# Low bits of float64 weights converted on ScalarE, and a planner that costs instructions by their spacing: attention, feed-forward block and gated block on one Trainium2 core

## The chip, the cores and the metric

The kernel runs on one core of a Trainium2 chip. The metric is the device time of one execution in microseconds (us). The times come from three runs; the profile comes from one more execution.

## What is computed

Three blocks follow one another on a batch of 4 sequences of 448 tokens, with 768 features (12 heads of 64). The weights and inputs of the second and third block are float64 in part.

```python
# attention, per head
scores = cap * np.tanh(scale * np.matmul(q, k.transpose(0, 1, 3, 2)) / cap)
attn = np.exp(scores - np.max(scores, axis=-1, keepdims=True))
attn = attn / (np.sum(attn, axis=-1, keepdims=True) + 1e-09)
x = np.matmul(attn, v)                            # then heads side by side
# feed-forward block
xn = (x - mu) / np.sqrt(var + 1e-06) * g_ln
x = x + np.maximum(xn @ w_ch1, 0.0) @ w_ch2       # 768 -> 3072 -> 768
# gated block
h = np.maximum(x @ w_in, 0.0)                     # 768 -> 1024
u, v = (h[..., :d_ff // 2], h[..., d_ff // 2:])
v_s = np.einsum('ts,bsd->btd', w_spatial, (v - mu) / np.sqrt(var + 1e-06)) + b_spatial[None, :, None]
out = (u * v_s) @ w_out
```

Weights reach the chip as pairs of 32-bit words, a low one and a high one, of a float64 number. The kernel makes a float32 of each pair by itself. Products are made of float32 split into two parts (a rounded one and the rest), with three matmuls for one product.

## The kernel before

The work on the four sequences is done in two passes of two sequences. In time order: attention of sequences 0 and 1 (some 0 to 115 us); the first feed-forward matmul of these two, with the attention of sequences 2 and 3 in between and the conversion of `w1` and `w2` (to about 350 us); the second feed-forward matmul, `y_seven`, which works with seven products in place of eight (to about 500 us); the gated block (to about 625 us); and the same two blocks for sequences 2 and 3, with weights that the first pass has converted and kept in memory (to the end).

No queue is written out by hand. `Recorder` notes every operation with an engine, a cost and a latency, in a program order; `Program.edges` finds what depends on what; `Program.order` gives each operation a due time, counted back from the TensorE work that needs it; `Program.plan` simulates the five queues (TensorE, VectorE, ScalarE, GpSimd, and SyncE, which issues all DMAs) with these costs and takes, for a free engine, the ready operation that is due first and has its buffers. The order in which the simulation takes the operations is the order in which they are emitted, so a change of any cost reorders every queue. An operation noted under `either()` has a second engine. The second engine takes it (`k` is above 0 in `pick`) only if its cost there is no greater than the wait that the simulation sees at the first engine, plus a bias: `BIAS` = 0.1 us, and -0.8 where the second engine is VectorE.

The cost in `Recorder.__getattr__` is a fixed part plus columns by a rate: for ScalarE 0.16 us (0.13 from PSUM) and 1200 columns per us, for VectorE 0.14 us and 960 (1920 for copies and `tensor_scalar` outside PSUM); the latency of both is 0, and `DELAY` = 0.13 us is added to every hand-over.

The conversion stands in `value`. A raw tile holds `n` pairs; `hi` and `lo` are its odd and even words, read with a stride of 8 bytes. ScalarE makes a rebased float of the high word (`Prelu` with a negative slope that keeps the sign), VectorE shifts this left by three bits (tile `t` seen as integers, `ti`), and VectorE ors in the three highest bits of the low word. Four early tiles of `w1` are given a `home` and go another way, with the sign put in by a third VectorE step. The float32 tile is then stored for the second pass, and `weight` or `y_seven` split it into two parts. In the trace the raw tiles are `w` (`w6`, `w4` in the code) and `w6m`, the converted ones `wr`, `wc` and `wcm`, and the split ones `wh`, `whm` and the like; `wr` is 768 columns wide, `wc` 512, `wcm` either. `hs` and `rs` are an activation and its split. Every operation is recorded by one line, L533, so rows are told apart by tiles.

Of the kernel before, what the change touches and what calls it, by code (L numbers as in the profile page):

```python
# [10 lines left out]
F32 = mybir.dt.float32  # L11
F32R = mybir.dt.float32r
I32 = mybir.dt.int32
ACTF = mybir.ActivationFunctionType
ALU = mybir.AluOpType

# [31 lines left out]
BIAS = 0.1  # L48
# [8 lines left out]


REBASE = 2.0 ** -112

EARLY = 4


class View:
# [17 lines left out]
    def __getattr__(self, name):  # L82
        return getattr(self.at, name)
# [127 lines left out]
class Program:  # L211
# [137 lines left out]
    def plan(self, due):  # L349

        n = len(self.ops)
# [12 lines left out]
        out = []  # L364
# [8 lines left out]
        def room(i):  # L373
            need = {}
            for b in bufs[i]:
                if b.tile is None:
                    need.setdefault(b.pool, set()).add(b)
            key = [(p, p.changes) for p in need]
            if blocked.get(i) == key:
                return False  # L380
            if all(p.fits(new) for p, new in need.items()):
                return True
            blocked[i] = key
            return False

        def reach():
            return max(spent + AHEAD, relief)

        def pick(e):


            q = ready[e]
            skipped = []
            found = None
            while q and found is None:
                d, i, k = heapq.heappop(q)
                if taken[i]:
                    continue
                if d > reach():
                    skipped.append((d, i, k))  # L400
                    break
                if k:
                    alt = self.ops[i][0]
                    home = alt[0][0]
                    wait = max(0.0, free[home] - now) if busy[home] else 0.0
                    for d2, i2, k2 in ready[home]:
                        if not taken[i2] and (d2, i2) <= (d, i) and not k2:
                            wait += self.ops[i2][0][0][1]
                    if alt[k][1] > wait + (BIAS if e != 'V' else -0.8):
                        skipped.append((d, i, k))  # L410
                        continue
                if not room(i):
                    skipped.append((d, i, k))
                    continue
                found = i, k
            for x in skipped:
                heapq.heappush(q, x)
            return found
# [5 lines left out]
        while True:  # L424
            for e in ready:
# [5 lines left out]
                i, k = found  # L431
# [6 lines left out]
                cost, latency = self.ops[i][0][k][1:3]  # L438
# [3 lines left out]
                if e == "D":  # L442
                    moved = max(moved, now + 1.1) + latency
                    latency = moved + 0.77 - now - cost
# [49 lines left out]
class Recorder:  # L494
# [3 lines left out]
    def __getattr__(self, method):  # L498
        fn = getattr(self.engine, method)

        def put(a):
            return a.place() if isinstance(a, View) else a

        def record(*args, **kw):
            out = kw["out"] if "out" in kw else args[0]
            ins = [a for a in list(args) + list(kw.values()) if hasattr(a, "tensor") and a is not out]
            n = out.free_size()
            latency = 0.0
            psum_in = any(a.space == bass.MemoryType.PSUM for a in ins)
            if self.name == "PE":  # L510
                cost = (n / 2400 + 0.0133) * kw["rhs"].ap[0][1] / 128
                if kw["rhs"].dtype == F32:

                    part = kw["rhs"].ap[0][1] * kw["out"].ap[0][1] / 128 ** 2
                    cost = (4 * n / 2400 + 0.004) * part + (0.004 if part < 1 else 0.0)
            elif self.name == "D":
                cost, latency = 0.5, 4 * out.size() / 360e3
            elif self.name == "A":
                cost = (0.13 if psum_in else 0.16) + n / 1200
                cost += 0.094 if hasattr(kw.get("scale"), "tensor") else 0.0  # L520
            elif self.name == "P":
                cost = 1.0 if "pow" in repr(args) + repr(kw) else 0.45 + n / 500
            elif method == "reciprocal":
                cost = 0.15 + n / 160
            elif method in ("tensor_copy", "tensor_scalar") and not psum_in:
                cost = 0.14 + n / 1920
            else:
                cost = 0.14 + n / 960
            if self.name == "V":
                cost += 0.06 * sum(hasattr(kw.get(k), "tensor") for k in ("scalar", "scalar1", "scalar2"))  # L530

            def call():
                fn(*(put(a) for a in args), **{k: put(a) for k, a in kw.items()})  # L533

            self.program.add(self.name, cost, latency, call, [out], ins)

        return record
# [3 lines left out]
def attn_ffn_gmlp_kernel(  # L541
# [17 lines left out]
    V, A, P, T, SP = (prog.engines[n] for n in ("V", "A", "P", "PE", "D"))  # L559
# [19 lines left out]
    def slots(name, n, shape, dt, pool=const):  # L579
# [7 lines left out]

    shapes = {"rb": ([128, 2, DH], F32R), "w6": ([128, DM, 2], I32), "es": ([128, 2, S], F32),
              "qk": ([128, 2 * S], F32), "vt": ([128, 512], F32), "acc": ([128, S], F32),
              "r": ([128, 2, S], F32R), "wr": ([128, DM + 24], F32), "wh": ([128, 2, DM], F32R),  # L590
              "wa": ([128, 2, HK], F32R), "wq": ([128, DM], F32), "pad": ([128, 24], F32), "gap": ([128, 48], F32), "w4": ([128, DH, 2], I32)}
    protos = {n: dram.tile(s, dt, name=f"proto_{n}") for n, (s, dt) in shapes.items()}
# [60 lines left out]
    def cp(o, a, engines=None):  # L653

        with prog.either():
            for e in engines or (V, A):
                if e is A:
                    A.activation(out=o, in_=a, func=ACTF.Copy)
                else:
# [24 lines left out]
    def ahead(kind, j):  # L684

        with prog.early():
            value(kind, j, pool=raw6[1])

    def value(kind, j, home=None, pool=wr):

        n = width[kind]
        if kind == "ws":
            t = hs.get()
            SP.dma_start(out=t, in_=source[kind][j])
        elif (kind, j) in kept:
            t = pool.get()[:, 0:n]
            SP.dma_start(out=t, in_=kept[kind, j])
        else:
            raw = raw6[0 if n > DH else 2].get()[:, 0:n]
            SP.dma_start(out=raw.rearrange("p n t -> p (n t)"), in_=source[kind][j].bitcast(I32))  # L700
            t = pool.get()[:, 0:n]
            ti = t.bitcast(I32)
            hi, lo = raw[:, :, 1], raw[:, :, 0]
            if home is None:
                A.activation(out=t, in_=hi.bitcast(F32), func=ACTF.Prelu, scale=REBASE, alpha=-(2.0 ** 32))
            else:
                with prog.either():
                    for e in (V, A):
                        if e is A:
                            A.activation(out=t, in_=hi.bitcast(F32), func=ACTF.Copy, scale=REBASE)  # L710
                        else:
                            V.tensor_scalar(out=t, in0=hi.bitcast(F32), scalar1=REBASE, scalar2=None, op0=ALU.mult)
            V.tensor_scalar(out=ti, in0=ti, scalar1=3, scalar2=None, op0=ALU.logical_shift_left)
            if home is not None:
                V.scalar_tensor_tensor(out=ti, in0=hi, scalar=-(1 << 31), in1=ti, op0=ALU.bitwise_and,
                                       op1=ALU.bitwise_or)
            V.scalar_tensor_tensor(out=ti, in0=lo, scalar=29, in1=ti, op0=ALU.logical_shift_right,
                                   op1=ALU.bitwise_or)
            if kind == "w2":
                if j % KD == 0:  # L720
                    kept2.append(dram.tile([128, KD, n], F32, name=f"kept_{kind}_{j}"))
                d = kept2[j // KD][:, j % KD]
            else:
                d = dram.tile([128, n], F32, name=f"kept_{kind}_{j}")
            kept[kind, j] = d
            SP.dma_start(out=d, in_=t)
        return t
# [59 lines left out]
    def expo(sc, e):  # L787
        A.activation(out=e, in_=sc, func=ACTF.Tanh, scale=qsc)
        A.activation(out=e, in_=e, func=ACTF.Exp, scale=capt)
        return e  # L790
# [17 lines left out]
    def split_s(i, t, cs):  # L808
# [7 lines left out]
        for c in cs:  # L816
# [14 lines left out]
            else:  # L831
                for half in range(2):
                    A.activation(out=e[:, half], in_=sc[half], func=ACTF.Tanh, scale=qsc)
                A.activation(out=e, in_=e, func=ACTF.Exp, scale=capt)
# [859 lines left out]
```

## Time and profile before

| | |
|---|---|
| median of 3 runs | 1033.38 us (1032.87 to 1036.49) |
| profiled execution, its own time | 1033.29 us |
| its span, first to last instruction | 1031.5 us |
| TensorE busy | 1009.9 us, 98% |
| VectorE busy | 828.4 us, 80% |
| ScalarE busy | 573.9 us, 56% |
| DMA queues' packets, share of 16 engines | 71.1% |

TensorE is the fullest engine. Its matmuls overlap and their ends are modelled, so time that is called busy can hold some waiting. Idle time of another engine costs nothing by itself.

### The profile page before, as it was taken

Reading aid. Unit: us, or ns where it says so; the run is one execution under the profiler, and the core shown is the slowest. Engines: PE = TensorE matmul, PEld = TensorE weight load, DVE = VectorE, ACT = ScalarE, POOL = GpSimd, SP = SyncE. Lnnn points to the kernel's source line nnn. Section 1 sums busy time; section 2 is a strip of 40 time slices with the busy share of each in tenths; the row PEclk is TensorE's granted clock in tenths of the full one; section 3 lists DMA queues with packets and bytes.
Section 4 is the critical chain, followed back from the end, with each engine's and each line's share of the span. In section 5 each row is a group of like instructions: output and inputs, shape, how many; then the busy total and the mean of one; then the engine's idle time right before and its main releaser. Section 6 shows DMA issues by size and latency. Waiting matters only on the chain.

```text
span 1031.5 us, 14887 instructions
## 1 busy us (share of the span) xinstructions
PE 1009.9 (98%) x5074; PEld 828.6 (80%) x5074; DVE 828.4 (80%) x1405; ACT 573.9 (56%) x903; POOL 17.3 (2%) x21
## 2 busy tenths in 40 slices
PE   7999999999999999999999999999999999999998
PEld 2333678788778888999789889899999999998987
DVE  6979998869677768989979889777788777778961
ACT  6989787787777444654545355444464322224612
POOL 0000000000000000000000210000000000000000
PEclk9999999999999999999999999999999999999999
DMA  7544689999999999999854233465699987502303
GB/s 248 159 120 155 205 288 372 354 396 370 363 372 347 315 317 336 389 393 363 296 179 156 50 129 109 151 198 189 224 366 347 361 272 223 189 21 86 99 21 118
DMA packets 162000, 248.71 MB, mean 241 GB/s; under 512 B 21970, under 2 KB 126084, under 8 KB 161924
## 3 DMA queue, kind: packets, MB, share of 16 engines
q1 hardware_dynamic: 161924, 247.76, 71.1%
q8 instruction: 40, 0.66, 0.3%
q14 instruction: 36, 0.29, 0.1%
HBM read 167.70 MB, written 80.01 MB: 240 GB/s over the span
## 4 chain that ended last, share of the span: by engine, by line
PE 72%; DMA 14%; DVE 8%; ACT 3%; issue 2%; SPq 1%; POOL 1%; DVEq 0%; ACTq 0%; POOLq 0%
PE bank L533 51%; PE two L533 20%; DMA hs<-h 3%; DMA wqm<-kept_w 3%; DMA hs<-inv 1%; DVE x L533 1%; DVE wh L533 1%; SPq L533 1%; DMA h<-hs 1%; DMA wrb<-kept_w 1%; DMA inv<-rc 1%; DVE hs L533 1%; DMA qk<-in_qk_dram 1%; ACT rs L533 1%; DVE rs L533 1%
## 5 line engine op out<-in xcount | busy, mean ns | idle before, releaser
L533 PE MATMUL bank<-rs,wh 128*128 128x448 f32 x1806 | 378.8, 363 | 3.7 <-DVE qkg L533 1.5
L533 PEld LDWEIGHTS bank<-rs,wh 128*128 128x128 f32 x1806 | 337.1, 187 | 33.4 <-issue 2.8
L533 DVE TENSOR_TENSOR rs<-hs,rs 128x448 fp32r<-128x448 f32 x159 | 95.1, 621 | 6.3 <-ACT rs L533 5.9
L533 PE MATMUL two<-rs,wh 128*128 128x448 f32 x420 | 94.9, 363 | 1.3 <-DVE rs L533 1.2
L533 DVE TENSOR_TENSOR wh<-wr,wh 128x768 fp32r<-128x768 f32 (+2 forms) x80 | 67.9, 855 | 27.1 <-ACT wh L533 26.9
L533 ACT ACTIVATE rs<-hs 128x448 fp32r<-128x448 f32 x123 | 68.4, 572 | 37.5 <-DMA hs<-h 36.7
L533 PEld LDWEIGHTS two<-rs,wh 128*128 128x128 f32 x420 | 78.5, 187 | 7.7 <-DVE rs L533 2.3
L533 ACT ACTIVATE wh<-wr 128x768 fp32r<-128x768 f32 (+2 forms) x70 | 53.3, 763 | 38.4 <-PE bank L533 16.5
L533 ACT ACTIVATE es<-es,capt 128x896 f32<-128x896 f32 x72 | 73.8, 1058 | 0.0
L533 ACT ACTIVATE es<-two,qsc 128x896 f32<-128x896 f32 x62 | 61.2, 1019 | 14.8 <-PE two L533 14.0
L533 PE MATMUL bank<-es,vt 128*64 128x448 f32 x288 | 63.0, 558 | 0.3 <-ACT hs L533 0.3
L533 DVE TENSOR_TENSOR es<-es,es 128x896 f32<-128x896 f32 x48 | 52.1, 1086 | 10.9 <-ACT es L533 10.6
L533 ACT ACTIVATE hs<-bank 128x448 f32<-128x448 f32 x61 | 32.6, 537 | 41.5 <-PE bank L533 39.0
L533 PEld LDWEIGHTS bank<-es,vt 128*64 128x64 f32 x288 | 17.6, 138 | 37.7 <-issue 28.6
L533 PE MATMUL two<-qk 64*128 64x448 f32 x168 | 41.8, 603 | 4.7 <-DMA qk<-in_qk_dram 4.2
L533 ACT ACTIVATE rs<-x 128x448 fp32r<-128x448 f32 x30 | 16.9, 575 | 41.3 <-DVE x L533 41.3
L533 ACT ACTIVATE hx<-bank 128x448 f32<-128x448 f32 x48 | 26.1, 543 | 22.0 <-PE bank L533 21.3
L533 PEld LDWEIGHTS two<-qk 64*128 64x128 f32 x168 | 14.5, 195 | 29.4 <-ACT es L533 15.4
L533 PE MATMUL two<-wh,rs 128*128 128x512 f32 x144 | 35.8, 395 | 0.0
L533 PE MATMUL bank<-rx,whb 128*128 128x448 f32 x144 | 32.7, 362 | 0.0
L533 PE MATMUL two<-rx,whb 128*128 128x448 f32 x144 | 32.7, 362 | 0.0
L533 PEld LDWEIGHTS two<-wh,rs 128*128 128x128 f32 x144 | 26.9, 187 | 6.8 <-DVE x L533 0.4
(210 smaller groups left out, 1774.1 us busy)
## 6 DMA issues: line engine op xcount, KB each, us to landing
hs<-h SPq DMA_DIRECT2D x168, 224.0 KB, 5.2
h<-hx SPq DMA_DIRECT2D x84, 224.0 KB, 5.0
w<-in_w_dram SPq DMA_DIRECT2D x24, 768.0 KB, 8.2
w<-in_w_dram SPq DMA_DIRECT2D x36, 512.0 KB, 6.3
wqm<-kept_w SPq DMA_DIRECT2D x30, 384.0 KB, 7.1
qk<-in_qk_dram SPq DMA_DIRECT2D x24, 448.0 KB, 6.1
h<-hs SPq DMA_DIRECT2D x48, 224.0 KB, 4.1
kept_w<-wr SPq DMA_DIRECT2D x24, 384.0 KB, 4.2
```

The lines of the kernel that those rows point to most:

```text
L533: fn(*(put(a) for a in args), **{k: put(a) for k, a in kw.items()})
```

## The change

Three things are changed.

In `value`, for tiles without a `home`, ScalarE reads the low word as an unsigned integer, scales it by about 2^-29, adds an offset of about -0.5 and writes the result back over the low word as an integer, which leaves the word's three highest bits. VectorE then shifts the rebased high word and ors this integer in, in one instruction. The tiles with a `home` keep their steps.

In `Recorder.__getattr__`, the fixed parts of the costs of ScalarE and VectorE become smaller and each gets a latency of 0.1 or 0.085 us. In `pick`, the bias of -0.8 for VectorE goes; it is 0.1 for all engines.

```diff
+TOP = 2.0 ** -29 * (1.0 - 2.0 ** -16)
+FLOOR = -0.5 + 7.5 * 2.0 ** -16
...
-                    if alt[k][1] > wait + (BIAS if e != 'V' else -0.8):
+                    if alt[k][1] > wait + BIAS:
...
             elif self.name == "A":
-                cost = (0.13 if psum_in else 0.16) + n / 1200
+                cost, latency = (0.063 if psum_in else 0.11) + n / 1200, 0.1
                 cost += 0.094 if hasattr(kw.get("scale"), "tensor") else 0.0
             elif self.name == "P":
                 cost = 1.0 if "pow" in repr(args) + repr(kw) else 0.45 + n / 500
             elif method == "reciprocal":
-                cost = 0.15 + n / 160
-            elif method in ("tensor_copy", "tensor_scalar") and not psum_in:
-                cost = 0.14 + n / 1920
+                cost = 0.12 + n / 160
             else:
-                cost = 0.14 + n / 960
+                fast = method in ("tensor_copy", "tensor_scalar") and not psum_in
+                cost, latency = 0.068 + n / (1920 if fast else 960), 0.085
...
-            V.tensor_scalar(out=ti, in0=ti, scalar1=3, scalar2=None, op0=ALU.logical_shift_left)
-            if home is not None:
+            if home is None:
+                A.activation(out=lo, in_=lo.bitcast(U32), func=ACTF.Copy, scale=TOP, bias=FLOOR)
+                V.scalar_tensor_tensor(out=ti, in0=ti, scalar=3, in1=lo, op0=ALU.logical_shift_left,
+                                       op1=ALU.bitwise_or)
+            else:
+                V.tensor_scalar(out=ti, in0=ti, scalar1=3, scalar2=None, op0=ALU.logical_shift_left)
                 V.scalar_tensor_tensor(out=ti, in0=hi, scalar=-(1 << 31), in1=ti, op0=ALU.bitwise_and,
                                        op1=ALU.bitwise_or)
-            V.scalar_tensor_tensor(out=ti, in0=lo, scalar=29, in1=ti, op0=ALU.logical_shift_right,
-                                   op1=ALU.bitwise_or)
+                V.scalar_tensor_tensor(out=ti, in0=lo, scalar=29, in1=ti, op0=ALU.logical_shift_right,
+                                       op1=ALU.bitwise_or)
```

## Rows read from the trace of the kernel before

**Rows 1.** The page's first part: busy us (share of the span) and instructions of each engine.

```profile
PE 1009.9 (98%) x5074; PEld 828.6 (80%) x5074; DVE 828.4 (80%) x1405; ACT 573.9 (56%) x903; POOL 17.3 (2%) x21
```

**Rows 2.** Stretches: start:end, us, busy (instructions) by engine, clock, DMA share, GB/s.

```profile
0.00:25.00 25.00, 18.51 (x74) 5.88 (x76) 14.92 (x23) 16.43 (x20) 0.81 (x9) 0.93 0.76 245
25.00:125.00 100.00, 97.56 (x478) 39.52 (x478) 88.17 (x146) 91.07 (x125) 0.00 (x0) 1.00 0.53 164
125.00:350.00 225.00, 225.00 (x1249) 175.82 (x1246) 182.69 (x294) 163.89 (x242) 2.20 (x2) 1.00 0.98 348
350.00:425.00 75.00, 70.73 (x347) 64.27 (x346) 58.02 (x84) 35.80 (x56) 0.00 (x0) 1.00 1.10 338
425.00:475.00 50.00, 50.00 (x252) 46.87 (x251) 45.70 (x72) 27.49 (x46) 0.00 (x0) 1.00 1.05 395
475.00:525.00 50.00, 48.05 (x224) 41.19 (x223) 47.64 (x84) 23.35 (x39) 0.00 (x0) 1.00 0.84 297
525.00:675.00 150.00, 147.31 (x722) 131.62 (x721) 127.40 (x234) 72.76 (x133) 12.03 (x8) 1.00 0.41 128
675.00:1025.00 350.00, 349.82 (x1731) 321.04 (x1730) 263.83 (x473) 142.03 (x243) 2.27 (x2) 1.00 0.58 195
1025.00:1031.52 6.52, 2.92 (x15) 2.39 (x13) 0.00 (x0) 1.09 (x2) 0.00 (x0) 1.00 0.22 82
```

**Rows 3.** The page's chain of waits that ended last, by engine.

```profile
PE 72%; DMA 14%; DVE 8%; ACT 3%; issue 2%; SPq 1%; POOL 1%; DVEq 0%; ACTq 0%; POOLq 0%
```

**Rows 4.** TensorE's waits from 470 to 525: us, times, longest.

```profile
PE two L533 <- DVE rs L533: 1.7, 3, 0.7
```

**Rows 5.** The chain of waits from 355 to 425, by line.

```profile
by line: DMA hs<-h 34.3%; DMA wqm<-kept_w 30.8%; PE bank L533 9.3%; SPq L533 7.4%; issue 4.2%; ACT rs L533 4.2%; DVE wh L533 3.1%; ACT wh L533 2.4%; DVE wqm L533 1.7%; DVE whm L533 1.4%; DVE rs L533 1.2%; DVEq L533 0.1%; ACTq L533 0.1%
```

**Rows 6.** TensorE's waits from 575 to 675, the longest.

```profile
PE bank L533 <- DVE qkg L533: 1.5, 1, 1.5
```

**Rows 7.** Conversion by groups: tiles, shape, count | busy us, mean ns | idle before.

```profile
L533 ACT ACTIVATE wc<-w 128x512 f32<-128x512 f32 x36 | 24.3, 675 | 10.0 <-DMA w<-in_w_dram 7.0 <-DVE wr L533 2.4 <-DVE rs L533 0.5
L533 ACT ACTIVATE wr<-w 128x768 f32<-128x768 f32 x20 | 17.8, 915 | 1.0 <-DVE es L533 0.5 <-DMA kept_w<-wr 0.4
L533 DVE TENSOR_SCALAR wc<-wc 128x512 int32<-128x512 int32 x36 | 15.2, 423 | 10.7 <-ACT wc L533 10.6
L533 DVE TENSOR_SCALAR wr<-wr 128x768 int32<-128x768 int32 x24 | 13.1, 555 | 0.4 <-ACT wr L533 0.2
```

**Rows 8.** ScalarE's splits of weights from 125 to 350.

```profile
L533 ACT ACTIVATE wh<-wr 128x768 fp32r<-128x768 f32 x21 | 17.6, 841 | 5.6 <-DVE wr L533 5.1 <-PE bank L533 0.4
```

**Rows 9.** Instructions that read raw tiles, 125 to 350: VectorE, ScalarE, clock, DMA.

```profile
125.00:350.00 225.00, 41.14 (x53) 37.65 (x51) 1.00 0.98 348
```

**Rows 10.** Conversion from 425 to 525: the Prelu and the shift.

```profile
L533 ACT ACTIVATE wcm<-w6m 128x512 f32<-128x512 f32 (+1 forms) x16 | 11.6, 723 | 15.8 <-DMA w6m<-in_w_u_dram 5.4 <-DVE x L533 3.7 <-DMA w6m<-in_w_v_dram 3.6
...
L533 DVE TENSOR_SCALAR wcm<-wcm 128x512 int32<-128x512 int32 (+1 forms) x16 | 7.3, 457 | 0.9 <-ACT wcm L533 0.7
```

**Rows 11.** VectorE in order of time: start us, us, what.

```profile
475.57 1.16 DVE L533 TENSOR_TENSOR rs<-hs,rs 128x448 fp32r<-128x448 f32 x2
476.65 0.95 DVE L533 TENSOR_TENSOR wh<-wqm,wh 128x768 fp32r<-128x768 f32 x1
477.52 0.55 DVE L533 TENSOR_SCALAR wcm<-wcm 128x768 int32<-128x768 int32 x1
```

**Rows 12.** ScalarE in order of time from 482: [idle before, and what ended it].

```profile
482.30 0.85 ACT L533 ACTIVATE whm<-wqm 128x768 fp32r<-128x768 f32 x1 [1.42 <-PE bank L533]
483.05 1.03 ACT L533 ACTIVATE rs<-hs 128x448 fp32r<-128x448 f32 x2
486.23 0.85 ACT L533 ACTIVATE wh<-wqm 128x768 fp32r<-128x768 f32 x1 [2.15 <-PE bank L533]
```

**Rows 13.** ScalarE's casts of activations from 425 to 525.

```profile
L533 ACT ACTIVATE rs<-hs 128x448 fp32r<-128x448 f32 x36 | 19.2, 569 | 1.8 <-DMA hs<-h 1.8
```

**Rows 14.** The same cast on VectorE, whole span.

```profile
L533 DVE CAST rs<-hs 128x448 fp32r<-128x448 f32 x36 | 13.7, 389 | 4.1 <-DMA hs<-h 4.1
```

## What the change will do to the time: a prediction

> **What bounds the kernel now.** I read the busy times first: TensorE 98%, VectorE 80%, ScalarE 56% [rows 1]. A busy TensorE isn't TensorE at its peak, so the second view is the table of stretches: where does TensorE fall idle at all, and who is full there [rows 2]? Its idle time is 6.49 us in the first 25 us (transfers and first scores), 3.60 us at the end (last copy and store), and in between 2.44 (25 to 125), 0 (125 to 350), 4.27 (350 to 425), 0 (425 to 475), 1.95 (475 to 525), 2.69 (525 to 675) and 0.18 (the rest), 21.6 us in all. The two ends are not touched by the change, so 11.5 us lie open: 1.1% of the time is all that a better order can return by this view. The chain that ended last says the same: 72% of it is TensorE [rows 3].
>
> Third, who ends the idle time. In 475 to 525 it is VectorE: three waits for the split of an activation, 1.7 us of the 1.95, while VectorE is busy 47.64 of 50 us and ScalarE 23.35 [rows 2, 4]. In 350 to 425 it is transfers: two kinds of load hold 65% of the chain there [rows 5]. In 25 to 125 both engines are near full (88.17 and 91.07 of 100) and the waits are scattered [rows 2]. In 525 to 675 one wait of 1.5 us for the gate on VectorE stands out [rows 6]. The granted clock is 1.00 (the 2.4 GHz level) in each stretch but the first, so it has no part in the sum [rows 2].
>
> **The change part by part.** (a) *Conversion.* 72 float64 weight tiles take this path: 56 of the 60 raw loads up to 350 us (four early tiles of w1 have a home of their own and keep the old steps) and the 16 of 425 to 525. Each had a ScalarE Prelu, a VectorE shift and a VectorE shift-and-or. The shift goes; the other stays one instruction of the same kind and size. Removed: 15.2 + 20 x 0.555 + 7.3 = 33.6 us of VectorE (the row of 24 shifts of wr holds the four early tiles too; the 7.3 are the 16 later tiles) [rows 7, 10]. Added: 72 ScalarE instructions that read 512 or 768 strided words, scale them and write them back as integers. No row shows that write. The nearest row is the Prelu of the same tile, which reads the same stride: 675 and 915 ns [rows 7]. Below, the same engine does 768 dense columns in 841 ns [rows 8]; above, I allow twice the Prelu, for a strided write. I take the Prelu: 36 x 0.675 + 20 x 0.915 + 11.6 = 54.2 us of ScalarE [rows 7, 10].
>
> Where these fall decides. In 125 to 350 ScalarE gets 37.65 us, the same as its 51 Prelus there [rows 9], and has 225 - 163.89 = 61.1 us idle; it comes to 201.5 of 225, 90%. TensorE has no idle time there, so this stretch can return nothing: VectorE's relief there is worth 0, and so is ScalarE's load as long as it stays under full. Its cover is the 61.1 us, and 21 splits of 0.841 us that the planner may hand to VectorE [rows 8]. In 425 to 525 VectorE sheds 16 shifts, 7.3 us, of which those between 476 and 498 stand right ahead of the splits that TensorE waits for; ScalarE, busy 50.84 of 100, takes 11.6 more [rows 2, 10, 11]. I give this the three waits: -1.7 us. What is late next there is the same split behind one shift-or: the bound is 0 to -1.95.
>
> The chain of one tile becomes longer: Prelu, Copy, VectorE instead of Prelu, shift, VectorE, by 0.675 - 0.423 = 0.25 us for 512 columns and 0.36 for 768 [rows 7]. The raw buffers (two of each width) are held so much longer, and the next load of a raw tile on SP's queue, with the loads of scores and activations queued behind it, is issued later when the planner meets no free buffer. One tile comes per 225/51 = 4.4 us against two buffers, so I cost it at 0.
>
> (b) *Costs by spacing.* The planner simulates the engines and emits each queue in that order. Its old cost of a 448-column VectorE step was 0.14 + 448/960 = 0.607 us, the new 0.535. The trace: two splits that follow one another take 1.16 us in all and the next starts 1.08 after the first, so 0.54 each, though one lasts 0.62 [rows 11]. ScalarE: two in 1.03 us at some 0.57 each, so 0.46 apart [rows 12, 13]; old 0.533, new 0.483. The new figures are nearer to the chip for both. Nothing is added or removed by this; all queues are reordered, SP's too, and only the open 11.5 us can move. The 4.27 us of 350 to 425 stay, since the bytes stay and the DMA share is 1.10 there. Of 2.44 (25 to 125) and 2.69 (525 to 675) I take half: -2.6 us, bounds 0 and -5.1. A worse order can also open waits; the unchanged bytes and constants say nothing for or against it, and I bound it by what the kernel shows in its worst open stretch for an engine reason, 2.44 us in 100, over 225 us of 125 to 350: +5.5.
>
> (c) *VectorE as second choice.* It took a ScalarE-home copy only if ScalarE's queue was at least 0.8 us longer than its own cost; now 0.1 us shorter is enough. In 425 to 525 36 such casts stand on ScalarE; VectorE does one in 389 ns against 569 [rows 13, 14]. If 7.3/0.389 = 19 of them come over, the relief of (a) in that stretch is gone. ScalarE is often idle ahead of these (1.42 and 2.15 us before the splits of two weights) [rows 12], which speaks for few; I cost it at 0, with +1.7 as its bound.
>
> Sum: 1033.29 (the profiled execution; 1.8 us more than its span, and 0.1 under the median 1033.38) - 1.7 - 2.6 = 1029.0 us. Its own range goes from all of 475 to 525, 25 to 125 and 525 to 675 returned (-7.1: 1026.2) to a third of the sum (1032).
>
> **The rivals.** *A, more is returned.* All 11.5 us close: 1021.8. It would need the transfers of 350 to 425 to be issued earlier; the share of 1.10 speaks against that, while matmuls spread out inside what counts as busy speak for it (478 in the 100 us from 25, 1731 in 350 later [rows 2]; they are of other kinds, so it can't be sized from counts). I allow it 2.8 us more, a quarter of the 11.5: 1019 is its far end.
>
> *B, no change.* ScalarE-home casts come to VectorE until it is as full as before, and reordering wins in one stretch what it loses in the next: 1033.3, between 1032 and 1036. For it: 98% busy. Against: measured spacings agree with the new figures. The Trainium skill (VectorE: DVE Perf Modes, The DRAIN you can't avoid) says that the next VectorE instruction doesn't start until the pipeline is empty; by that the old 0.607 would be nearer and (b) would be worth nothing. The starts 0.54 us apart speak against it in this kernel, so it adds nothing to this rival's chance.
>
> *C, slower: ScalarE becomes the bound in 125 to 350.* Its idle time is 61.1 us for 51 tiles, so it decides at 61.1/51 = 1.2 us for one integer Copy, or sooner where tiles come in clumps: it holds tanh, exp and the releases of PSUM banks, which TensorE waits for, in one queue. At 88 to 91% busy on both engines TensorE idles 2.44 us in 100 [rows 2]; over 225 us that is +5.5, and twice that for a strided write of double price: 1038.8 to 1044; I say 1040. For it: 90% expected load. Against: VectorE can take splits. The Trainium skill (ScalarE: Activation LUTs, Rules for kernel authors) tells to put multiplies and adds on VectorE and not on ScalarE; by that rule C is what should happen. The trace has ScalarE busy 56% and VectorE 80%, which is why I don't make it the forecast.
>
> The change not doing what it says (ScalarE writing something else than the integer in place) would not change the times above, only the values.
>
> **How the numbers follow.** Forecast 0.36, A 0.24, B 0.22, C 0.18. What a measurement of this kernel can tell from no change is about 0.5%, 5.2 us: faster is under 1028.2, slower over 1038.5. Faster: A and two fifths of the forecast, 0.24 + 0.14 = 0.38. Slower: nearly all of C, 0.17. Within: 0.45. The range leaves out the far halves of A and C: 1020 to 1040.
>
> **What would show it.** After the change the TENSOR_SCALAR rows of wc and wcm are gone, 72 ScalarE rows w<-w stand at 0.65 to 0.95 us, and VectorE's busy time falls by some 25 to 34 us less what casts it takes over; ScalarE's rises by less than 54. In 475 to 525 no wait for the split is left; 350 to 425 keeps some 4 us; 125 to 350 stays at 0. The prediction is wrong if TensorE falls idle in 125 to 350 on ScalarE's releases or the Copy is over 1.2 us (C), if casts on VectorE rise by 19 or more in 425 to 525 (B), or if the idle time of 350 to 425 goes (A).

## The result and the profile after

The changed kernel takes 1048.35 us (1046.82 to 1054.86, 6 runs) where the kernel before takes 1035.08 us (1032.87 to 1038.6, 6 runs): ratio 1.0136, 95% interval 1.0101 to 1.0172. It is slower, 19 us over the forecast and 8 us over the upper end of the range. The profiled execution took 1048.22 us with a span of 1046.5.

Page of the changed kernel, first part, the lines that answer to [rows 1] and [rows 3]:

```profile
PE 1015.6 (97%) x5074; PEld 830.7 (79%) x5074; DVE 847.5 (81%) x1451; ACT 554.9 (53%) x858; POOL 17.0 (2%) x20
...
PE 53%; DMA 24%; DVE 15%; issue 3%; ACT 3%; SPq 2%; POOL 1%; DVEq 0%; ACTq 0%; POOLq 0%
```

The span grew by 14.9 us. TensorE's idle time grew by 9.3 (30.9 for 21.6), and its busy time by 5.7 for the same 5074 matmuls. VectorE shed 72 shifts and yet has 46 instructions more; ScalarE got 72 Copies and has 45 fewer: some 118 operations that have both engines as alternatives moved from ScalarE to VectorE. VectorE is as full as before. In the chain of waits that ended last TensorE's share fell from 72% to 53%.

Stretches of the changed kernel, columns and stretches as in [rows 2]:

```profile
0.00:25.00 25.00, 18.79 (x68) 5.66 (x68) 14.97 (x23) 16.71 (x21) 0.81 (x9) 0.93 0.75 240
25.00:125.00 100.00, 95.79 (x470) 39.49 (x468) 84.69 (x139) 87.52 (x117) 0.00 (x0) 0.99 0.55 159
125.00:350.00 225.00, 223.30 (x1228) 171.01 (x1227) 177.04 (x271) 182.30 (x267) 3.14 (x2) 1.00 0.96 342
350.00:425.00 75.00, 71.49 (x353) 65.27 (x352) 62.63 (x99) 25.71 (x40) 0.00 (x0) 1.00 1.07 332
425.00:475.00 50.00, 49.33 (x245) 45.44 (x244) 46.12 (x74) 27.66 (x45) 0.00 (x0) 1.00 1.05 389
475.00:525.00 50.00, 49.61 (x241) 44.89 (x240) 47.67 (x83) 25.89 (x41) 0.00 (x0) 1.00 0.87 310
525.00:675.00 150.00, 144.81 (x702) 127.79 (x701) 127.53 (x242) 67.41 (x126) 10.86 (x7) 1.00 0.41 134
675.00:1025.00 350.00, 344.66 (x1692) 314.85 (x1691) 280.42 (x516) 120.42 (x205) 2.17 (x2) 1.00 0.58 192
1025.00:1046.45 21.45, 17.80 (x89) 16.34 (x88) 6.42 (x11) 1.26 (x2) 0.00 (x0) 0.97 0.37 133
```

Against [rows 2], TensorE's idle time by stretch: -0.3 in the first 25 us, +1.8 in 25 to 125, +1.7 in 125 to 350, -0.8, +0.7, -1.6 in 475 to 525, +2.5 in 525 to 675, and +5.2 in 675 to 1025. The largest part lies where no weight is converted any more. The later stretches don't hold quite the same work, since the kernel lags. The last tiles are converted by 533 us, and TensorE is not idle from 525 to 535 in either kernel, so all added idle time after 525 us is of another cause than the conversion's own instructions.

TensorE's waits in the changed kernel (us in all, times, longest), the five largest of the whole span:

```profile
PE two L537 <- DMA qk<-in_qk_dram: 4.2, 1, 4.2
PE two L537 <- ACT hs L537: 4.1, 3, 2.5
PE bank L537 <- DVE rs L537: 3.8, 5, 2.7
PE bank L537 <- DVE wh L537: 3.4, 4, 1.2
PE bank L537 <- ACT wh L537: 2.6, 3, 1.7
```

The first is the opening load, 4.2 us in the kernel before too. In the second and third, single waits of 2.5 and 2.7 us are new: the kernel before waits 0.5 us in all for `hs` with `two`, and its list has no wait of `bank` for `rs`. The three waits of [rows 4] for the split are gone.

Conversion and casts in the changed kernel, groups by tile and shape (columns as in [rows 7]):

```profile
L537 ACT ACTIVATE w<-w 128x512 int32<-128x512 uint32 x36 | 24.1, 673 | 0.0
...
L537 DVE CAST rs<-hs 128x448 fp32r<-128x448 f32 x59 | 22.7, 390 | 7.9 <-DMA hs<-h 7.8
...
L537 ACT ACTIVATE w<-w 128x768 int32<-128x768 uint32 x20 | 18.0, 904 | 0.0
```

The integer Copy costs 673 and 904 ns, as the Prelu of the same tile does (675 and 915 [rows 7]). The casts of `rs` on VectorE, in the whole span, rose to 59.

**Where the two large waits come from.** In both, an instruction that is ready stands in an in-order queue behind one that isn't. First ScalarE, the changed kernel at 966 us (start, us, instruction, times; in brackets the idle time before it and what ended it):

```profile
966.11 0.55 ACT L537 ACTIVATE hs<-bank 128x448 f32<-128x448 f32 x1 [0.88 <-PE bank L537]
969.35 0.63 ACT L537 ACTIVATE rbc<-vtc 128x512 fp32r<-128x512 f32 x1 [2.70 <-DVE vtc L537]
970.40 1.28 ACT L537 ACTIVATE rbc<-vtc 128x512 fp32r<-128x512 f32 x2 [0.42 <-DVE vtc L537]
971.59 0.53 ACT L537 ACTIVATE hs<-two 128x448 f32<-128x448 f32 x1
```

TensorE there:

```profile
968.91 0.76 PE L537 MATMUL bank<-rc,wh 128*128 128x448 f32 x3
972.16 2.55 PE L537 MATMUL two<-rs,wh 128*128 128x448 f32 x9 [2.49 <-ACT hs L537]
```

ScalarE idles 2.70 us for `vtc`, which VectorE normalises late, and the copy that frees the PSUM bank `two` waits behind the three splits. In the kernel before the same copy stands ahead of them:

```profile
958.78 0.55 ACT L533 ACTIVATE hs<-two 128x448 f32<-128x448 f32 x1 [1.25 <-PE two L533]
960.05 1.68 ACT L533 ACTIVATE rbc<-vtc 128x512 fp32r<-128x512 f32 x3 [0.72 <-DVE vtc L533]
```

Second VectorE, the changed kernel at 594 us:

```profile
593.80 3.67 DVE L537 SCALAR_TENSOR_TENSOR x<-x,g_t,rstd 128x448 f32<-128x448 f32 x6 [0.37 <-DMA rstd<-rstd]
598.06 3.66 DVE L537 SCALAR_TENSOR_TENSOR x<-x,g_t,rstd 128x448 f32<-128x448 f32 x6 [0.60 <-DMA rstd<-rstd]
601.64 0.62 DVE L537 TENSOR_TENSOR rs<-qkg,rs 128x448 fp32r<-128x448 f32 x1
```

TensorE there:

```profile
602.32 0.67 PE L537 MATMUL bank<-rs,wh 128*128 128x448 f32 x2 [2.70 <-DVE rs L537]
```

The split that TensorE wants stands behind twelve steps that a transfer released; in the kernel before, one such split and two steps of the gate (`qkg`) stand between these twelve. At about the same place of the work the kernel before waits 1.5 us for the gate [rows 6], a wait that the changed kernel doesn't have; so this place lost some 1.2 us and not all of the 2.70.

### The profile page after: what moved, and what is told of

It is laid out like the page before. It is cut to its first block, busy times and chain, and to the rows that moved or that the text cites. A ratio compares the mean times of both kernels' runs of the same rounds, so it can differ in the third digit from the quotient of the medians.

```text
span 1046.5 us, 14855 instructions
## 1 busy us (share of the span) xinstructions
PE 1015.6 (97%) x5074; PEld 830.7 (79%) x5074; DVE 847.5 (81%) x1451; ACT 554.9 (53%) x858; POOL 17.0 (2%) x20
## 4 chain that ended last, share of the span: by engine, by line
PE 53%; DMA 24%; DVE 15%; issue 3%; ACT 3%; SPq 2%; POOL 1%; DVEq 0%; ACTq 0%; POOLq 0%
PE bank L537 33%; PE two L537 20%; DMA hs<-inv 4%; DMA hs<-h 4%; DMA w<-in_w_dram 3%; DMA h<-hx 2%; DVE wh L537 2%; SPq L537 2%; DVE x L537 2%; DVE rs L537 2%; DMA qk<-in_qk_dram 2%; DVE hs L537 2%; DVE es L537 1%; DMA kept_w<-wr 1%; DMA wr<-kept_w 1%
## 5 line engine op out<-in xcount | busy, mean ns | idle before, releaser
L537 ACT ACTIVATE rs<-hs 128x448 fp32r<-128x448 f32 x100 | 55.9, 572 | 61.5 <-DMA hs<-h 50.7
L537 ACT ACTIVATE wh<-wr 128x768 fp32r<-128x768 f32 (+2 forms) x49 | 37.3, 760 | 24.1 <-DVE wr L537 13.0
L537 ACT ACTIVATE w<-w 128x512 int32<-128x512 uint32 (+1 forms) x56 | 41.6, 756 | 0.0
L537 DVE SCALAR_TENSOR_TENSOR wc<-wc,w 128x512 int32<-128x512 int32 x36 | 24.6, 686 | 17.1 <-ACT w L537 17.0
L537 ACT ACTIVATE rs<-x 128x448 fp32r<-128x448 f32 x26 | 14.7, 573 | 44.6 <-DVE x L537 44.3
L537 ACT ACTIVATE hs<-bank 128x448 f32<-128x448 f32 x53 | 28.0, 534 | 17.6 <-PE bank L537 13.4
L537 ACT ACTIVATE wc<-w 128x512 f32<-128x512 f32 x36 | 24.2, 672 | 18.7 <-DMA w<-in_w_dram 14.9
L537 ACT ACTIVATE whb<-wrb 128x768 fp32r<-128x768 f32 x23 | 19.4, 846 | 26.6 <-issue 18.7
```

## The experiments

Each ratio is against runs of the kernel before on the same chip, with its 95% interval.

**1. One step at a time.** The conversion alone, with the costs and the bias of before:

```diff
...
+                A.activation(out=lo, in_=lo.bitcast(U32), func=ACTF.Copy, scale=TOP, bias=FLOOR)
+                V.scalar_tensor_tensor(out=ti, in0=ti, scalar=3, in1=lo, op0=ALU.logical_shift_left,
+                                       op1=ALU.bitwise_or)
...
```

> Only the conversion is changed (integer Copy on ScalarE, one VectorE step); old costs and old bias in the planner. Order theory (the new waits come from the reordered queues, not from the conversion's load): within 4 us of the kernel before, 1030 to 1038, no new idle time of TensorE after 575 us. Load theory (rival C: ScalarE is made the bound from 125 to 350): 1042 or more, with TensorE idle in 100 to 350. Luck theory (any edit makes another plan, and plans differ by several us): anywhere from 1028 to 1046, with new waits at places that have nothing to do with the conversion.

The new costs alone:

```diff
-                cost = (0.13 if psum_in else 0.16) + n / 1200
+                cost, latency = (0.063 if psum_in else 0.11) + n / 1200, 0.1
...
+                cost, latency = 0.068 + n / (1920 if fast else 960), 0.085
```

> Only the planner's costs are changed (spacing instead of duration); the old conversion, the old bias of -0.8. Order theory, if the costs make it: 1043 to 1050, with waits of TensorE at 575 to 650 and 950 to 1005 as in the kernel after. Order theory, if the bias makes it: 1030 to 1038. Load theory: 1030 to 1036. Luck theory: anywhere from 1028 to 1046.

The new bias alone:

```diff
-                    if alt[k][1] > wait + (BIAS if e != 'V' else -0.8):
+                    if alt[k][1] > wait + BIAS:
```

> Only the bias of VectorE as second engine is changed from -0.8 to 0.1; old costs, old conversion. Order theory, if the bias makes it: 1042 to 1050, with the casts on VectorE up by 20 or more. Order theory, if the costs make it: 1030 to 1038. Load theory: 1030 to 1036. Luck theory: anywhere from 1028 to 1046.

And the costs and the bias together, without the conversion:

> New costs and new bias, old conversion: the kernel after without its conversion. Order theory: 1043 to 1050, about as slow as the kernel after, since the stretches 575 to 650 and 950 to 1005 hold no conversion. Load theory: 1030 to 1037. Luck theory: anywhere from 1028 to 1050.

Measured: the conversion alone 1043.81 us, 1.0072 (1.0051 to 1.0093); the costs alone 1062.15 us, 1.0256 (1.0216 to 1.0296); the bias alone 1036.78 us, 0.9996 (0.9973 to 1.0019); costs and bias 1052.2 us, 1.016 (1.0107 to 1.0212). The costs, which add and remove no work, are the loss, larger alone than the whole change and above every range that was expected. The bias alone came out as expected if the costs make the loss. The conversion alone missed the order theory's 1030 to 1038 and has both signs of the load theory: over 1042, and TensorE idle 4.9 us in 125 to 350. But 2.9 us of these are one wait for the load of scores (of the kind shown below) and only 1.6 end at ScalarE; experiments 2 and 7 put the same Copies on ScalarE without that idle time. In the kernel with the new costs alone TensorE idles 495 - 482.32 = 12.7 us from 525 us on, for 2.9 in 525 to 1025 before [rows 2]. Stretch of that kernel:

```profile
525.00:1020.00 495.00, 482.32 (x2332) 434.63 (x2331) 394.46 (x727) 201.45 (x350) 14.15 (x10) 0.99 0.55 178
```

One of its waits is for a load. DMA issues of the kernel with the new costs at 130 us:

```profile
130.72 0.32 SPq L537 DMA_DIRECT2D var_t<-var  x1
131.13 0.38 SPq L537 DMA_DIRECT2D qk<-in_qk_dram  x1
```

And its TensorE:

```profile
134.51 0.97 PE L537 MATMUL bank<-qk 64*64 64x448 f32 x4 [2.94 <-DMA qk<-in_qk_dram]
```

The load of the next scores is issued behind a small transfer that itself waited 2.9 us for another one, and TensorE waits 2.94 us for it. The place on SP's queue is not what is new, though. In the kernel before the load stands behind the same transfer, which there waits 4.0 us:

```profile
126.44 0.32 SPq L533 DMA_DIRECT2D var_t<-var  x1
127.42 0.35 SPq L533 DMA_DIRECT2D qk<-in_qk_dram  x1
```

Its TensorE has other matmuls first and takes the next scores 18 us after that load was issued:

```profile
127.31 7.70 PE L533 MATMUL bank<-rs,rs 128*128 128x448 f32 x36
145.86 0.98 PE L533 MATMUL bank<-qk 64*64 64x448 f32 x8
```

What the new plan changed is TensorE's own order: it puts matmuls that need the load ahead of matmuls that don't. The kernel with the conversion alone does the same, with the same wait of 2.94 us.

**2. The conversion in an unchanged order.** To price step (a) by itself, the Copy is noted with the cost of the shift that it replaces, under VectorE, and is issued to ScalarE; the queues of TensorE and SP are then those of before, instruction by instruction.

```diff
...
+                def low(lo=lo):
+                    x = lo.place()
+                    nc.scalar.activation(out=x, in_=x.bitcast(U32), func=ACTF.Copy, scale=TOP, bias=FLOOR)
+
+                prog.add("V", 0.14 + n / 1920, 0.0, low, [ti], [ti])
...
```

> The conversion of the kernel after in the exact queue order of the kernel before: the planner still counts a VectorE shift, and the integer Copy is issued on ScalarE at its place. TensorE's and SP's queues are the same as before, instruction for instruction. Load theory: slower by 5 us or more, with TensorE idle between 100 and 350. Order theory and luck theory: within 3 us of before; the prediction's step (a) says 1.7 us faster, with the waits for the split at 475 to 525 gone.

Measured: 1038.22 us, 1.002 (1.0006 to 1.0034). Its page and three stretches:

```profile
PE 1010.5 (98%) x5074; PEld 829.2 (80%) x5074; DVE 801.6 (78%) x1333; ACT 614.6 (59%) x975; POOL 17.4 (2%) x21
```

```profile
125.00:350.00 225.00, 224.75 (x1248) 176.30 (x1241) 162.06 (x239) 194.09 (x293) 2.56 (x2) 1.00 0.98 347
425.00:525.00 100.00, 98.77 (x481) 89.42 (x480) 88.06 (x140) 59.73 (x102) 0.00 (x0) 1.00 0.96 350
470.00:525.00 55.00, 53.77 (x256) 47.25 (x255) 49.25 (x82) 31.10 (x53) 0.00 (x0) 1.00 0.88 316
```

And TensorE's waits in 470 to 525:

```profile
PE two L536 <- DVE rs L536: 1.2, 3, 0.5
```

Exactly 72 instructions changed engine (VectorE 1405 to 1333, ScalarE 903 to 975). ScalarE is at 86% in 125 to 350 and TensorE idles 0.25 us there: rival C's mechanism doesn't occur. But the three waits for the split shrink only from 1.7 to 1.2 us, and TensorE's busy time in 425 to 525 rises by 0.7 (98.77 for 98.05). The whole is 0.2% slower, some 2 us, with an interval that just leaves out 1: in an unchanged order the conversion costs a little, and its forecast gain of 1.7 us isn't seen in the total.

**3. What does any new plan cost?** Three edits of the kernel before that mean nothing for the work change one constant of the planner each: the delay between engines, VectorE's fixed cost, and how far the planner looks ahead.

```diff
-    DELAY = 0.13
+    DELAY = 0.131
```

> The kernel before with the planner's hand-over delay 0.131 in place of 0.130 us: an edit without meaning, which still moves several hundred places in the queues. Order theory (the new costs are at fault as such): within 3 us of before. Luck theory (any other plan loses what this one happens to avoid): 5 us slower or more, with a wait at 115 to 155 or at 950 to 1005.

```diff
-                cost = 0.14 + n / 960
+                cost = 0.141 + n / 960
```

> The kernel before with VectorE's fixed cost 0.141 in place of 0.140 us for all but copies: an edit without meaning that moves more places than the one of the delay. Order theory: within 3 us of before. Luck theory: 5 us slower or more.

```diff
-AHEAD = 28
+AHEAD = 28.3
```

> The kernel before with the planner's look-ahead 28.3 in place of 28 us: a third edit without meaning, for the spread of the old costs. From the other two (1039.5 and 1042.0 against 1035.6): 1035 to 1043, with another set of waits. Above 1046 the spread by luck alone would reach the kernel after.

Measured: 1042.0 us, 1.0064 (1.0041 to 1.0088); 1039.51 us, 1.0028 (1.0003 to 1.0054); 1037.47 us, 1.0001 (0.9986 to 1.0016). A thousandth of a microsecond in one constant costs up to 0.64% (two runs). The conversion alone, at 1.0072, can't be told from that, for the intervals overlap; the new costs, at 1.0256, are far outside.

**4. Which costs?** VectorE's alone:

```diff
-                cost = 0.14 + n / 960
+                fast = method in ("tensor_copy", "tensor_scalar") and not psum_in
+                cost, latency = 0.068 + n / (1920 if fast else 960), 0.085
...
```

> The new costs for VectorE alone; ScalarE's costs, the bias and the conversion as before. Margin theory (the old costs, longer than the spacing, left room in each queue; with it gone, waits that the plan doesn't see reach TensorE): if VectorE's margin is what counts, 1050 to 1065, near the 1062 of both costs. Luck theory (any replan costs 0 to 8 us, the new costs have no part of their own): 1034 to 1044.

ScalarE's alone:

```diff
-                cost = (0.13 if psum_in else 0.16) + n / 1200
+                cost, latency = (0.063 if psum_in else 0.11) + n / 1200, 0.1
```

> The new costs for ScalarE alone; VectorE's costs, the bias and the conversion as before. Margin theory, if ScalarE's margin is what counts: 1050 to 1065. Margin theory, if VectorE's is (VectorE is the fuller engine): 1036 to 1046. Luck theory: 1034 to 1044.

Measured: 1051.62 us, 1.0159 (1.0123 to 1.0194) and 1052.43 us, 1.0134 (1.0076 to 1.0193). Either half is enough.

Nor is it the share of the two engines. First parts of the pages with ScalarE's new costs alone, with the costs 0.04 us above the old (experiment 5), and with the bias alone (experiment 1):

```profile
PE 1017.5 (97%) x5074; PEld 832.0 (79%) x5074; DVE 826.9 (79%) x1402; ACT 575.8 (55%) x906; POOL 23.5 (2%) x21
PE 1019.2 (97%) x5074; PEld 834.3 (79%) x5074; DVE 828.2 (79%) x1397; ACT 576.1 (55%) x910; POOL 19.7 (2%) x22
PE 1009.0 (98%) x5074; PEld 828.4 (80%) x5074; DVE 843.4 (82%) x1445; ACT 552.2 (54%) x864; POOL 16.6 (2%) x20
```

The first two keep VectorE's and ScalarE's counts of before (1405 and 903) within 8 and are 1.3 and 1.4% slower; the third moves some 40 operations to VectorE and loses nothing. The new costs come with new latencies, and no run changes one of the two by itself.

**5. Is it lost margin?** My theory after these runs: the old costs were too high by 0.05 to 0.07 us and so left room for steps that come late; the loss grows with the room taken away. Costs halfway between old and new, and costs 0.04 us above the old, both for both engines (VectorE's main line is shown of each):

```diff
-                cost = 0.14 + n / 960
+                cost, latency = 0.104 + n / 960, 0.04
...
```

> The kernel before with the costs halfway between old and new (0.104 for VectorE, 0.135 and 0.097 for ScalarE, latencies 0.04 and 0.05). Margin theory, by degrees: halfway between before and the new costs alone (1062), or the mean of the new-cost plans: 1043 to 1052. Threshold or luck: 1035 to 1043, as the edits without meaning.

```diff
-                cost = 0.14 + n / 960
+                cost = 0.18 + n / 960
...
```

> The kernel before with costs 0.04 us above the old ones for both engines: more room than before. Margin theory by degrees: no slower than the edits without meaning, 1030 to 1040, perhaps faster than before. If the old costs are merely a point to which everything else was fitted, it's as slow as the other side: 1045 to 1055. Luck theory: 1035 to 1043.

Measured: halfway 1047.1 us (1041.43 to 1050.34), 1.0101 (1.0075 to 1.0128); above 1052.43 us, 1.0143 (1.0062 to 1.0224). Halfway agrees; more room should have been as good as the old costs or better, and it is as bad as the new ones. The theory falls: a departure to either side is worse.

**6. Repairs of the changed kernel.** More hand-over delay in the planner (0.2), the other look-ahead (28.3), and the right size for `bn_stats`, whose cost the planner takes from its 6 output columns (0.074 us by the new cost) though it reads 512 and lasts some 0.69 us; this chain comes before the normalised `vtc` that ScalarE waits for in the view above. (Two copies of `vtc` and two splits of weights come before it on VectorE too, so what makes it late isn't settled.)

```diff
-    DELAY = 0.13
+    DELAY = 0.2
```

> The kernel after with the planner's hand-over delay 0.20 in place of 0.13 us: every dependent step is planned 0.07 us later, engines are planned as full as in the kernel after. Margin theory, if room in the chains is enough: 1036 to 1043. If the room has to be on the engines' own time: 1045 to 1055. Luck theory: 1040 to 1056, no more than another draw.

```diff
-AHEAD = 28
+AHEAD = 28.3
```

> The kernel after with the planner's look-ahead 28.3 in place of 28 us: the spread of the new costs under an edit without meaning. If the new costs have a part of their own: 1046 to 1056. If the kernel after is just an unlucky draw: 1035 to 1044.

```diff
+                n = max(n, max(x.free_size() for x in ins)) if method == "bn_stats" else n
```

> The kernel after, but the planner counts a bn_stats by the 512 columns that it reads (0.60 us) and not by the 6 that it writes (0.074 us). Theory of the optimistic plan: ScalarE's queue holds the copy that frees the bank at 971.6 behind two splits that wait for this chain, since the plan takes the chain for shorter than it is; with the right cost that wait (2.5 us, and the clock's fall behind it) goes: 1043 to 1046. Luck theory: the time moves by some us in either direction, and the wait at the normalisation may stay or not.

Measured: 1048.56 us, 1.0107 (1.008 to 1.0134); 1044.8 us, 1.0073 (1.0039 to 1.0108); 1048.39 us, 1.0111 (1.008 to 1.0142). The second falls between its two ranges and decides nothing between an own part of the costs and a bad draw. The last one mends its place but not the time, for which 1043 to 1046 was expected. ScalarE of the kernel with the right size of `bn_stats`:

```profile
975.02 0.55 ACT L538 ACTIVATE hs<-two 128x448 f32<-128x448 f32 x1 [1.25 <-PE two L538]
975.98 1.15 ACT L538 ACTIVATE rbc<-vtc 128x512 fp32r<-128x512 f32 x2 [0.42 <-DVE vtc L538]
```

The copy is ahead of the splits again, and no wait of TensorE is left between 950 and 1010; the total stays. Other orders changed with it: TensorE's waits for split weights from VectorE (`wh`) are 7.7 us in that kernel, 3.4 in the changed one.

**7. The change without its costs.** Conversion and bias, with the costs of before; as a diff of the changed kernel:

```diff
-                cost, latency = (0.063 if psum_in else 0.11) + n / 1200, 0.1
+                cost = (0.13 if psum_in else 0.16) + n / 1200
...
-                cost, latency = 0.068 + n / (1920 if fast else 960), 0.085
+                cost = 0.14 + n / 960
```

> The kernel after with the old costs: the new conversion and the new bias alone. If the new costs are the part that makes it slow: 1035 to 1044, as the other plans by the old costs. If the conversion or the bias is: 1045 to 1050.

Measured: 1033.26 us, 0.9975 (0.9953 to 0.9996): the loss is gone, and the time is a little below the kernel before and below the 1035 to 1044 that was expected. Its page and a stretch:

```profile
PE 1009.5 (98%) x5074; PEld 831.6 (81%) x5074; DVE 825.5 (80%) x1391; ACT 585.9 (57%) x918; POOL 16.0 (2%) x20
```

```profile
425.00:525.00 100.00, 99.67 (x485) 90.27 (x484) 88.19 (x143) 58.12 (x95) 0.00 (x0) 1.00 0.94 343
```

TensorE's busy time in 425 to 525 is 99.67 for 98.05 before. To see whether the 0.25% is a draw, the same kernel with two constants of experiment 3, the look-ahead of 28.3 and the delay of 0.131:

> The conversion and the added bias, planned by the old costs, as in the fastest kernel so far (ratio 0.9975), with one constant changed that means nothing for the work: the planner looks ahead 28.3 instead of its old value. If that kernel's 0.25% is a draw among orders, this one lies anywhere from 1033 to 1043 us, as the edits without meaning in the kernel before did (ratios 1.000 to 1.006). If it is the merit of the two edits, it stays at or below 1036 us, ratio at most 1.000.

> The same kernel of the conversion and the bias by the old costs, with the planner's delay between engines at 0.131, the edit that cost the kernel before 0.64%. A draw among orders: 1033 to 1043 us. Own merit: at most 1036 us.

Measured: 1034.61 us, 0.9983 (0.9959 to 1.0007), and 1034.47 us, 0.9983 (0.9964 to 1.0002), beside 1036.56 us for the kernel before. All three lie some 0.2% below the kernel before, one interval wholly so, two just reaching 1. That is what the theory of an own merit expected, but a draw was given 1033 to 1043 and covers all three as well; each interval by itself is hardly distinct from no change.

## Why the prediction was wrong, point by point

**Step (b), costs by spacing: wrong in sign; this is the failing step.** It gave -2.6 us with an end of +5.5. The costs alone measured +2.56%, some 26 us; taking them out of the whole change moves it from 1.0136 to 0.9975. The step argued that a figure nearer to the chip gives a better order. The premise holds in the trace of after: VectorE's split starts at 601.64 and the step behind it at 602.18, 0.54 us apart as the new cost says. (The Trainium skill, VectorE: DVE Perf Modes, The DRAIN you can't avoid, on which the prediction drew, adds in the same paragraph that a next instruction that isn't held starts earlier; the trace agrees with that half.) What doesn't follow is the order. The planner leaves other things as they are: the 6 columns of `bn_stats`, the durations of transfers, a greedy choice of what is due first. A step that arrives late by 2 us holds up what stands behind it in an in-order queue, as the views of 594 and 966 us show, and a plan that takes matmuls before their load is there makes TensorE wait, as at 130 us. All eight plans with other costs (the changed kernel, its three repairs, costs alone and with the bias, and each engine's) and the two in experiment 5 measured 1.007 to 1.026; the four with old costs and the new bias 0.9975 to 0.9996; the five with old costs (one of them changed by 0.001 us) and the old bias 1.0001 to 1.0072. So all ten plans by other costs lie at or above the worst of nine by the old ones (the nearest, 1.0073 and 1.0072, can't be told apart). That the costs are the loss is shown; why each of the other cost sets does worse isn't settled: margin as a matter of degree fell with the costs above the old. That the old values are ones to which the planner's other constants fit is my reading, and no run shows it.

The bound was at fault as well. "+5.5" came from the idle share of the kernel's worst open stretch, that is from the order that was already there. The edits without meaning move the time by up to 0.64%, 6.6 us, so a bound for any edit that reorders all queues can't be smaller than that.

**Step (a), conversion: price right, load put too high, gain not shown.** The Copy took 673 and 904 ns for 675 and 915. In the unchanged order ScalarE's busy time grew by 40.7 us for 54.2, and VectorE's fell by 26.8 for 33.6: the sums added durations, while instructions in a row overlap, as step (b) itself had read from the splits. So the planned 90% of ScalarE in 125 to 350 became 86%, and 125 to 350 returned nothing and cost nothing there. The -1.7 us for the three waits was 0.7 less idle time in 425 to 525 with the queues unchanged, and the total was 2 us longer: VectorE was still busy 49.25 of 55 us there, so the split remained late behind other steps. With the queues planned anew by the old costs, TensorE's busy time in 425 to 525 rose by 1.6 us (experiment 7), in a total that a draw can explain. The Trainium skill (ScalarE: Activation LUTs, Rules for kernel authors) would keep a multiply and add on VectorE; that 72 of them on ScalarE in place of a VectorE shift made the unchanged order 0.2% slower (0.06 to 0.34) is no evidence against that rule.

What (a) costed at nothing, the longer chain of a tile and SP's queue, is within the 2 us (0.6 to 3.5) of the unchanged order. Another price was left out: each such edit makes a new plan, and the conversion alone with the old bias came out at 1.0072.

**Step (c), bias: right.** 0 forecast; the bias alone is 0.9996. In 425 to 525 the casts of `rs` on VectorE went from 5 to 13 in the changed kernel, below the 19 that would have cancelled (a). They did come over elsewhere: 118 operations in all changed sides, so rival B's first half (VectorE as full as before, 81%) happened.

**The rivals.** Slower came true, but not by C: ScalarE has 182.30 of 225 us in 125 to 350, the Copy takes 0.67 us, far from 1.2, and of TensorE's 1.70 us of idle time there 0.5 end at ScalarE. A is out: the idle time of 350 to 425 shrank from 4.27 to 3.51 but came back elsewhere. B's second half (what is won in one stretch is lost in the next) named the right mechanism with too small a spread: it spoke of a sum near zero.

**The clock.** "It has no part in the sum" was wrong once stalls grew; see below.

## What to carry to other kernels

An edit of the costs in a planner that orders all queues is an edit of every queue: price it by what edits without meaning do to the same kernel (here 0 to 0.64%), and make it a change of its own, apart from the change that it accompanies. Durations closer to the chip are by themselves no argument for a better order: here costs nearer to the measured spacing and costs further from it both gave slower plans. Look for what stands at the head of an in-order queue and is late, and compare the same place in the kernel before, where the same late step may cost nothing. Where TensorE is 98% busy and only 11.5 us lie open, a plan drawn anew has more to lose than to win.

## What the hardware showed unexpectedly

After waits TensorE's granted clock fell to its lower level for a stretch. Stretches of the changed kernel around the two falls (columns as in [rows 2]; the sixth figure, ahead of the DMA share, is the granted clock):

```profile
120.00:123.60 3.60, 2.01 (x8) 0.87 (x8) 3.60 (x7) 1.73 (x5) 0.00 (x0) 1.00 0.40 146
123.60:127.00 3.40, 3.40 (x10) 1.21 (x8) 3.30 (x8) 2.65 (x4) 0.00 (x0) 0.51 0.99 319
127.00:131.00 4.00, 4.00 (x25) 1.10 (x21) 4.00 (x9) 3.46 (x7) 0.00 (x0) 0.99 0.60 243
970.00:973.50 3.50, 1.34 (x7) 1.26 (x8) 3.50 (x13) 2.96 (x6) 1.16 (x1) 1.00 0.00 0
973.60:976.90 3.30, 3.30 (x11) 2.94 (x10) 3.30 (x6) 2.31 (x4) 0.00 (x0) 0.50 0.35 109
977.00:980.00 3.00, 3.00 (x16) 2.81 (x16) 2.34 (x5) 0.53 (x1) 0.00 (x0) 1.00 0.02 7
```

Ahead of each fall TensorE was busy 2.01 of 3.60 and 1.34 of 3.50 us; then it is fully busy at 0.51 and 0.50, the 1.2 GHz level, and 11 matmuls take 3.30 us where the next 16 take 3.00, some 1.2 us lost in the second fall. So a wait of 2.49 us cost about half as much again after it was over, and that part is booked as busy time. (Ahead of the first fall stand two shorter waits, of 0.53 and 1.06 us.) Between its first 20 and its last 2 us the kernel before has no such fall, the changed one two, the one with the new costs alone five, with TensorE's busy time at 1021.6 us for 1009.9. The falls follow the waits, and they aren't the loss by themselves: the fastest kernel, of experiment 7, has two as well. Two falls of some 1.2 us are less than half of the 5.7 us by which the changed kernel's busy time grew; the rest isn't explained.

The runs of one kernel can spread more than one expects: the kernel with VectorE's new costs alone lay between 1046.24 and 1057.19 us, so a few tenths of a per cent need repeated runs beside the kernel before.
